# q and k of an attention block loaded whole, from DRAM tiles that span all chunks, in a new order of work

## The chip, the cores and the metric

The kernel runs on one core of a Trainium2 chip. The metric is the device time of one execution in microseconds (us), the lower the better. The engines are named as in the profile: PE (TensorE, matmuls), PEld (its weight loads), DVE (VectorE), ACT (ScalarE), POOL (GpSimd) and SP (SyncE, which here issues every DMA). L249 is line 249 of the kernel before.

## The reference, cut to what matters

```python
# x [1, 2048, 448], wqkv [448, 3*448], wo [448, 448]
# w_gate, w_up [448, 1792], w_down [1792, 448]; 16 heads of 28, window 256
qkv = split_heads(layernorm(x) @ wqkv)          # q, k, v: [16, 2048, 28]
scores = q @ k.T * 28 ** -0.5                   # masked: 0 <= row - col < 256
o = softmax(where(mask, scores, -1e9)) @ v
h = x + merge_heads(o) @ wo
y = layernorm(h)
h2 = h + (gelu(y @ w_gate) * (y @ w_up)) @ w_down
```

All inputs and the output are float32. The kernel splits each float32 operand of a matmul into a high and a low part (ACT makes the high part at L252, DVE or POOL the low part at L255) and adds the three products that matter, so one product of 448 rows takes 11 matmuls.

## The kernel before, in words

The 2048 rows lie in 16 tiles of 128 rows, four tiles to a chunk of 512. The 16 heads lie in four groups of four. A block is one group in one chunk: B from 0 to 15, in two passes of two groups each; chunk c comes after chunk c - 1 within a pass.

**Start.** SP loads the tiles of x (L510), the weights of v in two halves (L583) and those of q and k (L609). Each tile of x is normalised (DVE, POOL), transposed on PE (L320) and split into `xT`. Products of `xT` and the weights of v follow (L249, 128x224). Where PE would be idle at the start, transposes of the identity are issued as fillers (L1315); nothing reads them.

**Projection of q and k** (`project_tile`). For a group and a chunk, 11 matmuls 128x512 fill one PSUM bank, ACT and DVE split it into a high and a low part, and DMAs write the parts to a DRAM tile: two bands in one transfer of 448 KB (L656) and the third in one of 224 KB (L657). A tile of q or k has the shape [112, 3, 512]: 4 heads of 28 rows, three bands (high and low, in an order that makes one product of 84 rows out of the three), 512 columns. Part of k of the last group travels along in pieces of 16 rows (64 and 32 KB).

**Loads** (`loads`, `get`, L678). They bring q and k of a block into SBUF as [84, 4, columns], 84 rows for each of four heads. The buffers `rq` and `rk` are double: block B uses number B % 2. `rk` holds the 256 columns of the chunk before and the 512 of its own. Before, a block takes two loads of q and two of its own k, each of 256 columns (84x4x256, 336 KB), and, if c > 0, one load of the last 256 columns of k of the chunk before. That makes 76 loads of 336 KB, 32 of q and 44 of k.

**Attention of a block.** Scores on PE (L249, `bank<-ring 84*128`, for each head and each tile of 128 queries), their maxima on DVE (L701), the maxima turned round through PE (L728) and back to SBUF, the scores once more with the maximum taken off (L249, `128*128`, out 128x384 or less: called the second scores below), exp on ACT (L775), masking on POOL (L788), the product with v on PE (L807, `29x...`), then wo. The second scores are the last readers of the block's `rq` and `rk`.

**FFN.** From about 306 us on PE has only the products of the FFN and of the last output.

**What sets the order.** The kernel is first recorded as a list of operations with their data; a table of numbers at the end of the file (PLAN) then says in which order each is issued, which PSUM bank it takes and how many fillers go where. No scheduler moves anything afterwards. All DMAs are on SP's one queue and are issued in its order: a transfer whose data or buffer isn't ready holds up all behind it. Eight completion semaphores are used in turn, so a DMA also waits for the eighth before it.

Of the kernel before, what the change touches and what calls it, by code (L numbers as in the profile page):

```python
# [9 lines left out]
F32 = mybir.dt.float32  # L10
# [8 lines left out]
NG = 4  # L19
# [33 lines left out]
MOVED = 16  # L53
QUICK = 4
# [81 lines left out]
def block_kernel(ctx: ExitStack, tc, x, wqk_in, wv_in, wo_in, ffn_in, halves_in, out):  # L136
# [10 lines left out]
    def f(ap):  # L147
# [25 lines left out]
    qk_d = [[[dram.tile([GF, 3, 512], F32, name=f"{'qk'[i]}{g}_{c}") for i in range(2)] for c in range(CS)]  # L173
            for g in range(NG)]
# [461 lines left out]
    def project_tile(p, c, m):  # L636
# [21 lines left out]
        put(slice(0, GF), qk_d[g][c][s], ("d", g, s, c), s, 1)  # L658
        put(slice(GF, 128), qk_d[NG - 1][c][1][16 * m:16 * m + 16], ("d", NG - 1, 1, c, m), 1, 0.15)
# [8 lines left out]
    def loads(B):  # L668
        g, c = block(B)
        u = B % 2  # L670

        def get(s, cc, lo, n, at, key):
            src = qk_d[g][cc][s].rearrange("(j p) b t -> (p b) j t", j=4)[:, :, lo * 128:(lo + n) * 128]
            dst, tok = (rk, "rk") if s else (rq, "rq")
            rd = [(("d", g, 1, cc, m), i) for m in range(WT) for i in range(2)] if s and g == NG - 1 else \
                [(("d", g, s, cc), i) for i in range(2)]
            rd += [("zk" if s else "zq", u, i) for i in range(2)]
            dma(key, 246 * n, lambda: nc.sync.dma_start(f(dst[u][0:3 * DH, :, at * 128:(at + n) * 128]), src),  # L678
                rd, [(tok, u, at + i) for i in range(n)])
# [641 lines left out]
    "c-pOZW3+5L)McEV?QGSxZQHhO+qP}nwr$(CZ5w^wx%KY%`cIG1qkGh-IxES_%3O2J<Rl1C00992aKHeHXfc2zY!cazBCLOYQN%cout22EBP|f&"  # L1321
    "`A-{1{{HEK5iJxM4@O1-k)!`uJaQ(CjP`Hu9}9;)K_rHM5d722B0m3E|KRzvE{(KFI4X+t=8<UrMaTc5_!9|7BIN&B2Sr9BVI(k|+n*MWj0GaU"
    "@IPz(&&Z!l{)s>%W5Y<sU^s6a5f?{{{P94M8K6j1e<GsrY#!+gB6H$l)ch}A6lQ`%VuxXN{)-SrdgI7Z9yy95bHIN+VC2Z3N`gove`><Qys~gr"
    "VR$VR#skAPj6{sW(O6_Yf7W1OE&Sn|MA|US00=V)!ZSb^`=1sJNBx(FKQ*V3xv+3;P?&WTRul{83Bs6pWZ%E>`QLu{w=RDwhQr*kzh53%8~&Fw"
    "5S|Ca8pmPu;6LpA$q|N8;{T|dhqL^5?jK$K?+E^Ifx`*{f1~lRPX6tOVJ{G_G7A6Y;a%`QY_f1%9I3y5IpblSfv`?+*zdnP4*yj#3;VOb9HYO="
    "{i7-vjspMgN*MO#VNOw4-TbdwSR_Z_KlOoOB=B!c{<jt=%o_X8YUr=mAJ+b;6@||v9Nvrnvz!00{_kl5|LzJHRws(oKaM<ycsO$qd8V<jZcyYX"
    "4Obh4D~rQx|LX_C=>9zs{vAQ#)9|11fBXL5{r>lL|Nq7Pzw^T&VT2VY!ipWqNUTWxr-<;?K}wJfq>7l49T*@!hzC-G#2^Yt4|0V5PoFd(CddUc"
    "fM_5GNCq;3v>*iX01qSq=|J-T%*_j;gPb5L$OLkO%Ag9!2daW<zz5Yq4WNLUAT!7hl7bi@%YWvy1_eMH&=#}<?Lh~S6$sD~bOHq<JUWA!unQ;z"
    "x`JAuHmCzk&<)fD^+93K0H~lL2tXsy7&HM*K{L=CXrKis0a}8=U<hahro*8i5s+XQhzo{;5nu+K1((2)U=)}QM}sk78LS7!0t-w5-N8~g6&QFN"
    "=mDmIB49e0180EoU?!La955Tq0TVz^Fc+2urNE>JRCB>{I1$)j9#{ZZz@=arFmW#s4bKP5L2s}EBmjNDLbwRbg9|`$uq0x}N-!U;0xRJ{&=;%*"  # L1330
    "YrrDd4{QS#?hm$u0bnCs1#P?-o&*wS53L1j;U;(*tOEmq3wD6La5Y>HqT|hQAM8!m!9k!H*a>3b^>9B-igtnBz`>`$7PtZK0Y$+9xESmO`@mK>"
    "8SDpZ;5K*woB`XRi(}%xgd-2f!VjT>0(=mDf<E2>Kf|5yAov1z!LP6nsRa6w4d5FbL3YFM@Fd&=AHhT56nqT(lSA+{+z3MWFc4@nh=LEpA8->m"
    "0)N8TxFm>*kHRD12|Na$!ZYw0EDerB6`h4A;B%NBzkui9OL!i>f*0UxcoAL%aquPZ29^UEa7O$K#>bc7d#Ite@G|@jGvO<+JkZfQco|dxFF<B|"
    "1!Rd3{V0+ZR|E#S3a^7~cr?k56W|*l5rpU^_z15-6UD_>!3TI9TBr=T2BM(&Fb9r@ZL}5KfKNa|92Mon(GWs6VJ>_NJ^};CZ5SPmBu~K|h>=8N"
    "$Xyr%Jq85bgE3Jed>_U_x4{E=9t<Q7x&v;4S6~pi0AeE_-2#>I5K;xd1{5X6RdEtLn1oO@TpcHdXTeZ%4lwivxab2IOOAm!s0O|Z-hu?MCLTtT"
    ";#xQ%{0NfaxM&=?2Zj?5b;aXJHyohk_&BJICz2F69-2T>;&&hw?vCT5)c6^A57OWyuntaw(&GDI5=ns4;Vs|+sEeP2qo4<Ff**o}C^P&7GQytt"
    "GZ=}oz@)Gjo=ke<OfV%(jQZeIuqmEGzJO-<8z=y?!oIi&EC|1XemFPIgNwqvI3KQu^W*Oz8*GjX;NPGz{sHRa{+LD_*NM<iP!Q*Xzd%D=2)Drb"
    "VN1+l16&w$SPC}6MX&-PEDc-Xq8LF9o&c?}fI74whBj=2lOq+j#RLXW!ge?WOF$Dwf$gyaU04zp$0cw{Y(Ni|!ck!t+yR%yWpFfD7N>{FkPpk@"
    "@;C#mfQ#W|up&+i3&H5H5>5w;!Opl0EDSs1>@YPPfQ!QzuoEr|hvGD_988JI!yGUL$_XpLTyPj3h%3S2I5!-DW5SWRA{>lI;Z$fU$pc5@)MyMI"
    "f~S#mC@+i!)1bF>I!TYl;@Ge`Ob%PX86+*L569t_a3&dqv!Pj}0jv(QquFE*sS0brxnv&6fvUmzWIWD^YQhDiGR%N#!3j7M%807KqvROLjE<9u"  # L1340
# [170 lines left out]
```

## Time and profile before

| | |
|---|---|
| time, three runs | 675.41, 675.41, 675.98 us; median 675.41 us |
| the profiled execution's own time | 675.42 us |
| its span in the profile | 673.7 us |
| PE busy | 662.4 us (98%), 4074 matmuls |
| DVE, ACT, POOL busy | 511.0, 406.9, 325.1 us |
| loads of q and k | 32 and 44, 336 KB each |
| granted TensorE clock | 1.00 in every stretch to 660 us |

The span is the stretch from the first to the last recorded instruction; 1.7 us of the time lie outside it. "Idle before, releaser" is the time in which an engine had nothing running, and the event that ended it. SPq, POOLq and the like are the sequencers that issue DMAs. The chain of waits goes back from the last instruction, at each step to what released it.

### The profile page before, as it was taken

What the parts mean: (1) busy time and instruction counts of PE and PEld (TensorE: products, weight loads), DVE (VectorE), ACT (ScalarE), POOL (GpSimd) and SP (SyncE); (2) the same over time, 40 slices, a digit from 0 to 9 for tenths busy, and PEclk for the clock granted to TensorE, in tenths of its full rate; (3) what the DMA queues carried; (4) which work ended last, traced back from release to release, by engine and by line L of the source; (5) the groups of instructions that cost most, each with busy time, mean ns of one, the idle gap of its engine ahead of it and who ended that gap; (6) DMA issues with size and microseconds to landing.
All of it is one profiled execution on the core that took longest, in us unless ns stands there. A gap on an engine that the chain in (4) does not pass through costs nothing.

```text
span 673.7 us, 12051 instructions
## 1 busy us (share of the span) xinstructions
PE 662.4 (98%) x4074; PEld 591.8 (88%) x4074; DVE 511.0 (76%) x1287; ACT 406.9 (60%) x793; POOL 325.1 (48%) x506
## 2 busy tenths in 40 slices
PE   7999999999999999999999999999999999999997
PEld 7998888888888888778999899999999989999996
DVE  7887888988778889868897879777775466465464
ACT  4767767787557778976455565556534454543531
POOL 6712445464345458865414654654444563453320
PEclk9999999999999999999999999999999999999999
DMA  8787866666566788643544434323021324122102
GB/s 296 204 257 234 272 203 180 210 190 196 153 188 212 209 207 227 157 112 86 140 108 102 102 96 119 103 91 93 20 71 53 122 68 119 54 67 55 64 15 109
DMA packets 97814, 93.73 MB, mean 139 GB/s; under 512 B 39064, under 2 KB 86360, under 8 KB 97752
## 3 DMA queue, kind: packets, MB, share of 16 engines
q1 hardware_dynamic: 97752, 92.96, 47.3%
q8 instruction: 32, 0.52, 0.3%
q14 instruction: 30, 0.25, 0.1%
HBM read 63.05 MB, written 29.88 MB: 138 GB/s over the span
## 4 chain that ended last, share of the span: by engine, by line
PE 91%; DVE 3%; DMA 2%; SPq 1%; issue 1%; POOL 1%; ACT 1%; DVEq 0%; POOLq 0%
PE bank L249 84%; PE bank L807 6%; DVE bank L701 1%; DMA ring<-k 1%; DMA pp<-in_wv_dram 1%; DMA q<-proj 1%; POOL proj L255 1%; PE bank L320 1%; PE bank L728 0%; DVE mhl L721 0%; ACT pp L775 0%; SPq L657 0%; ACT ring L252 0%; POOL pp L788 0%; SPq L510 0%
## 5 line engine op out<-in xcount | busy, mean ns | idle before, releaser
L249 PE MATMUL bank<-xT,proj 128*128 128x512 f32 x648 | 183.4, 386 | 0.0
L701 DVE CUSTOM_DVE_ANT_0 bank<-bank,mask 128x384 f32<-128x384 f32 (+2 forms) x256 | 131.5, 550 | 23.5 <-PE bank L249 18.4
L249 PE MATMUL bank<-ring 84*128 84x384 f32 (+7 forms) x629 | 140.1, 311 | 1.7 <-DMA ring<-k 0.7
L249 PEld LDWEIGHTS bank<-xT,proj 128*128 128x128 f32 x648 | 118.5, 190 | 12.4 <-issue 0.4
L249 PE MATMUL bank<-xT,ring 128*128 128x512 f32 x508 | 127.5, 379 | 0.0
L249 PE MATMUL bank<-ring,proj 128*128 128x448 f32 x617 | 125.3, 353 | 0.0
L249 PEld LDWEIGHTS bank<-ring,proj 128*128 128x128 f32 x617 | 116.5, 189 | 2.8
L249 PEld LDWEIGHTS bank<-ring 128*128 128x128 f32 (+1 forms) x629 | 106.1, 190 | 12.5 <-ACT pp L775 2.0
L775 ACT ACTIVATE pp<-bank 128x384 f32<-128x384 f32 (+1 forms) x212 | 103.9, 534 | 21.8 <-PE bank L249 18.2
L249 PEld LDWEIGHTS bank<-xT,ring 128*128 128x128 f32 x508 | 95.9, 189 | 12.2 <-DVE v L1022 0.3
L788 POOL TENSOR_SCALAR_AFFINE_SELECT pp<-pp 128x512 f32<-128x512 f32 x120 | 73.3, 639 | 63.1 <-ACT pp L775 61.2
L249 PE MATMUL bank<-proj,xT 128*128 128x224 f32 x352 | 72.6, 268 | 1.1 <-ACT proj L252 1.1
L946 POOL TENSOR_TENSOR raw<-raw 64x128 f32<-64x128 f32 (+1 forms) x110 | 54.9, 510 | 28.7 <-DMA raw<-in_halves_dram 17.1
L249 PEld LDWEIGHTS bank<-proj,xT 128*128 128x128 f32 x352 | 59.4, 191 | 2.3 <-ACT proj L252 1.3
L255 POOL TENSOR_TENSOR ring<-raw,ring 128x256 fp32r<-128x256 f32 (+2 forms) x48 | 43.1, 906 | 35.1 <-ACT ring L252 34.2
L1022 DVE TENSOR_TENSOR v<-v,bank 128x512 f32<-128x512 f32 x48 | 32.8, 683 | 30.6 <-PE bank L249 26.0
L252 ACT ACTIVATE ring<-bank 8x512 fp32r<-8x512 f32 x64 | 37.0, 584 | 24.5 <-PE bank L728 23.6
L255 DVE TENSOR_TENSOR proj<-v,proj 128x512 fp32r<-128x512 f32 (+1 forms) x57 | 38.6, 691 | 17.3 <-ACT proj L252 17.0
L249 PE MATMUL bank<-wos,ohl 128*128 128x448 f32 x192 | 49.3, 359 | 0.1
L252 ACT ACTIVATE proj<-v 128x512 fp32r<-128x512 f32 (+1 forms) x57 | 32.9, 593 | 26.2 <-DVE v L1048 13.6
L1078 DVE TENSOR_TENSOR hres<-bank,hres 128x448 f32<-128x448 f32 x64 | 37.5, 616 | 12.7 <-PE bank L249 12.6
L946 POOL TENSOR_TENSOR v<-raw 128x256 f32<-128x256 f32 x22 | 18.0, 818 | 57.2 <-DMA raw<-in_halves_dram 30.1
(118 smaller groups left out, 1028.9 us busy)
## 6 DMA issues: line engine op xcount, KB each, us to landing
ring<-k SPq DMA_DIRECT2D x44, 336.0 KB
raw<-in_halves_dram SPq DMA_DIRECT2D x22, 640.0 KB
ring<-q SPq DMA_DIRECT2D x32, 336.0 KB
q<-proj SPq DMA_DIRECT2D x15, 448.0 KB
k<-proj SPq DMA_DIRECT2D x11, 448.0 KB
ge<-in_halves_dram SPq DMA_DIRECT2D x20, 224.0 KB
xn<-xn SPq DMA_DIRECT2D x64, 64.0 KB
hres<-in_x_dram SPq DMA_DIRECT2D x16, 224.0 KB
```

The costliest lines, as they stand in the source:

```text
L249: nc.tensor.matmul(o.rearrange("p (t h) -> p t h", h=2), w, mixed(m), **how)
L252: nc.scalar.activation(dst, src, AF.Copy)
L255: (eng or nc.vector).tensor_sub(dst, src, f(hi))
L320: nc.tensor.transpose(bank[b.k][:, n * 128:(n + 1) * 128], xn[i2][:, o:o + 128], ident)
L701: nc.vector.tensor_tensor_reduce(at, at, plain(mask[:, o:384]), 1.0, -BIG, OP.add, OP.max, mx[i // 2][:, i % 2, j:j + 1])
L775: nc.scalar.activation(pp[:, j:j + per, o * 128:o * 128 + n].rearrange("p j (h t) -> p j h t", h=2), bank[b.k][:, 0:n * per].rearrange("p ...
L788: nc.gpsimd.affine_select(a, a, pattern=[[0, 4], [-cm, 128]], compare_op=op_, fill=0.0, base=0, channel_multiplier=cm)
L807: nc.tensor.matmul(bank[b.k][32 * j:32 * j + DH + 1, lo * 128:(hi + 1) * 128], v[:, 4 * c - 2 + m, g % 2, j, :], pp[:, j, at[m] * 128:(at[ ...
L946: op("pool", 0.14 + n * 0.00215, 0.18 + n * 0.00215, key, lambda: nc.gpsimd.tensor_tensor(out, a, b, op=OP.subtract), [*ar, *br], w, port= ...
L1022: op("dve", 0.605, 0.702, key, lambda: nc.vector.tensor_tensor(plain(out), plain(a), unmixed(bank[bs[i].k]), op=OP.add), ar, w, bs[i])
L1078: op("dve", 0.533, 0.626, key + 3 * q + 3, lambda t=t, b=banks[q]: nc.vector.tensor_tensor(plain(hres[:, t, :]), unmixed(bank[b.k][:, 0:D] ...
```

## The change

The DRAM tiles of q and of k span all chunks: one tile [112, 3, 2048] for each group and each of q and k, in place of one [112, 3, 512] for each chunk too. A chunk writes and reads its columns of it. The write of two bands puts down 112x2x512, in pieces of 2 KB a row and band, where it was 112x1024 in one piece of 4 KB. A block's q comes in one load 84x4x512 (672 KB, pieces of 2 KB) in place of two 84x4x256 (pieces of 1 KB), its own k likewise; the load of k of the chunk before stays as it was. There are 44 loads: 16 of q and 28 of k. With that, PLAN is a new table: on every engine operations stand in another order, and the banks have other numbers. The numbers in `LOADS` and the keys belong to the search for the table; once PLAN is there they move nothing. The arithmetic is the same.

```diff
+LOADS = {2: 492, 4: 560, 6: 760}
+ROWS = (((0, 0, 4, 0), (1, 0, 4, 0)), ((1, -2, 2, 0), (0, 0, 4, 0), (1, 0, 4, 0)))
...
-    qk_d = [[[dram.tile([GF, 3, 512], F32, name=f"{'qk'[i]}{g}_{c}") for i in range(2)] for c in range(CS)]
-            for g in range(NG)]
+    qk_d = [[dram.tile([GF, 3, S], F32, name=f"{'qk'[i]}{g}") for i in range(2)] for g in range(NG)]
...
+        at = slice(512 * c, 512 * c + 512)
         def put(rows, d, name, s, size):
-            dma(key, 458 * size, lambda: nc.sync.dma_start(d[:, s:s + 2], both[rows]), tok, [(name, 0)])
-            dma(key, 229 * size, lambda: nc.sync.dma_start(d[:, 2 - 2 * s], both[rows, 0]), tok[0:1], [(name, 1)])
+            dma(key, 458 * size, lambda: nc.sync.dma_start(d[:, s:s + 2, at], both[rows]), tok, [(name, 0)])
+            dma(key, 229 * size, lambda: nc.sync.dma_start(d[:, 2 - 2 * s, at], both[rows, 0]), tok[0:1], [(name, 1)])
...
-        def get(s, cc, lo, n, at, key):
-            src = qk_d[g][cc][s].rearrange("(j p) b t -> (p b) j t", j=4)[:, :, lo * 128:(lo + n) * 128]
+        def get(s, t, n, key):
+            lo = 4 * c + t
+            src = qk_d[g][s].rearrange("(j p) b t -> (p b) j t", j=4)[:, :, lo * 128:(lo + n) * 128]
...
-            dma(key, 246 * n, lambda: nc.sync.dma_start(f(dst[u][0:3 * DH, :, at * 128:(at + n) * 128]), src),
+            dma(key, LOADS[n], lambda: nc.sync.dma_start(f(dst[u][0:3 * DH, :, at * 128:(at + n) * 128]), src),
                 rd, [(tok, u, at + i) for i in range(n)])
         key = 16 * B - (8 if B > 1 else 24)
-        if c:
-            get(1, c - 1, 2, 2, 0, key)
-        for i in range(0, 4, 2):
-            get(0, c, i, 2, i, key + 4 * i)
-            get(1, c, i, 2, 2 + i, key + 4 * i)
+        for s, t, n, k in ROWS[c > 0]:
+            get(s, t, n, key + k)
...
 PLAN = (
-    "c-pOZW3+5L)McEV?QGSxZQHhO+qP}nwr$(CZ5w^wx%KY%`cIG1qkGh-IxES_%3O2J<Rl1C00992aKHeHXfc2zY!cazBCLOYQN%cout22EBP|f&"
+    "c-pPFbGRqD7B*TzC8?y4Qg++6ZEM=L-P5*hyL;NUZQItgZM*yS*}Z4Zx&Ph!eBZ98s=~G2^{zLmU$&;{8r84{HKb|3O5oS?KV|%@9sVklUv2c)"
...
```

The order at the places that the prediction speaks of. A row is a line of the kernel, the operation, its output and inputs, the output's shape, and how many follow one another; the lines of the changed kernel are one to four higher.

First SP at the start of the program, before. `in_x`, `in_wv` and `in_wqk` are x and the weights.

```order
L510 DMA hres<-in_x_dram 128x448 x4
L583 DMA pp<-in_wv_dram 128x448
L609 DMA raw<-in_wqk_dram 128x512
L583 DMA pp<-in_wv_dram 128x448
L510 DMA hres<-in_x_dram 128x448
L609 DMA raw<-in_wqk_dram 128x512
L510 DMA hres<-in_x_dram 128x448 x10
```

The same place in the changed order:

```order
L511 DMA hres<-in_x_dram 128x448 x3
L584 DMA pp<-in_wv_dram 128x448
L511 DMA hres<-in_x_dram 128x448
L584 DMA pp<-in_wv_dram 128x448
L610 DMA raw<-in_wqk_dram 128x512
L511 DMA hres<-in_x_dram 128x448 x7
L610 DMA raw<-in_wqk_dram 128x512
```

Both halves of the weights of v now stand ahead of the first weights of q and k; the fourth tile of x stands behind the first half.

PE at the same place, before: fillers (`bank<-ident`), transposes of x (`ident,xn`), and the first products for v (`proj,xT`).

```order
L1315 MATMUL bank_141<-ident 128x128 x15
L320 MATMUL bank_136<-ident,xn_80 128x128 x4
L1315 MATMUL bank_141<-ident 128x128 x5
L320 MATMUL bank_135<-ident,xn_80 128x128 x4
L249 MATMUL bank_134<-proj,xT 128x224 x7
L320 MATMUL bank_139<-ident,xn_85 128x128 x4
L1315 MATMUL bank_141<-ident 128x128 x5
L249 MATMUL bank_140<-proj,xT 128x224 x8
```

And in the changed order:

```order
L1319 MATMUL bank_117<-ident 128x128 x19
L321 MATMUL bank_110<-ident,xn_80 128x128 x4
L1319 MATMUL bank_117<-ident 128x128 x4
L321 MATMUL bank_117<-ident,xn_80 128x128 x4
L1319 MATMUL bank_116<-ident 128x128 x5
L250 MATMUL bank_112<-proj,xT 128x224 x7
L321 MATMUL bank_115<-ident,xn_85 128x128 x4
L1319 MATMUL bank_116<-ident 128x128
L250 MATMUL bank_110<-proj,xT 128x224 x8
```

Five fillers moved from behind the first seven products for v to before them, and one is left behind.

SP again, at the loads of block 2 (q0 and k0 are group 0), before; q0_1 is q of group 0 in chunk 1.

```order
L678 DMA ring_77<-k0_1_89 84x4x256
L657 DMA k3_2_115<-proj_78 16x512
L678 DMA ring_77<-q0_1_88 84x4x256
L860 DMA raw_79<-in_wo_dram 128x448
L656 DMA k3_2_115<-proj_78 16x1024
L656 DMA k0_2_91<-proj_78 112x1024
L657 DMA k0_2_91<-proj_78 112x512
L657 DMA k3_2_115<-proj_78 16x512
L678 DMA ring_77<-k0_1_89 84x4x256
L678 DMA ring_77<-q0_1_88 84x4x256
```

The same loads in the changed order:

```order
L660 DMA k3_93<-proj_78 16x512
L659 DMA k3_93<-proj_78 16x2x512
L659 DMA q0_86<-proj_78 112x2x512
L685 DMA ring_77<-q0_86 84x4x512
L685 DMA ring_77<-k0_87 84x4x512
L660 DMA k3_93<-proj_78 16x512
L659 DMA k0_87<-proj_78 112x2x512
```

The two pairs of loads, with six other transfers between them, are one pair of twice the size.

PE at the first scores of block 2, before: a product of block 0 with v (`pp,v`), the turned maxima (`one,mhl`), products for later blocks, and in the last row but one the first score of block 2.

```order
L807 MATMUL bank_138<-pp,v 29x384 x8
L807 MATMUL bank_138<-pp,v 29x256 x4
L807 MATMUL bank_138<-pp,v 29x128 x4
L728 MATMUL bank_137<-one,mhl_148 72x128
L249 MATMUL bank_135<-xT,proj 128x512 x2
L728 MATMUL bank_141<-one,mhl_150 72x128
L249 MATMUL bank_135<-xT,proj 128x512 x3
L249 MATMUL bank_134<-ring 128x384
L249 MATMUL bank_140<-proj,xT 128x224
```

In the changed order, from two rows behind that product to the first score of block 2, the last row:

```order
L250 MATMUL bank_116<-proj,xT 128x224
L250 MATMUL bank_110<-ring 128x128
L250 MATMUL bank_116<-proj,xT 128x224
L250 MATMUL bank_111<-xT,proj 128x512
L732 MATMUL bank_113<-one,mhl_124 72x128
L250 MATMUL bank_116<-proj,xT 128x224 x2
L250 MATMUL bank_111<-xT,proj 128x512
L250 MATMUL bank_116<-proj,xT 128x224 x3
L250 MATMUL bank_111<-xT,proj 128x512
L732 MATMUL bank_112<-one,mhl_126 72x128
L250 MATMUL bank_116<-proj,xT 128x224
L250 MATMUL bank_110<-ring 128x384
```

More work stands between the product with v and the first score of block 2: products for v, and scores of block 1.

More of the change, by code (lines that the diff above doesn't have):

```diff
@@ L670, in loads @@
         u = B % 2
-        def get(s, cc, lo, n, at, key):
-            src = qk_d[g][cc][s].rearrange("(j p) b t -> (p b) j t", j=4)[:, :, lo * 128:(lo + n) * 128]
+        def get(s, t, n, key):
+            lo = 4 * c + t
+            src = qk_d[g][s].rearrange("(j p) b t -> (p b) j t", j=4)[:, :, lo * 128:(lo + n) * 128]
             dst, tok = (rk, "rk") if s else (rq, "rq")
-            rd = [(("d", g, 1, cc, m), i) for m in range(WT) for i in range(2)] if s and g == NG - 1 else \
-                [(("d", g, s, cc), i) for i in range(2)]
+            at = t + 2 * s
+            rd = []
+            for cc in range(lo // 4, (lo + n + 3) // 4):
+                rd += [(("d", g, 1, cc, m), i) for m in range(WT) for i in range(2)] if s and g == NG - 1 else \
+                    [(("d", g, s, cc), i) for i in range(2)]
             rd += [("zk" if s else "zq", u, i) for i in range(2)]
-            dma(key, 246 * n, lambda: nc.sync.dma_start(f(dst[u][0:3 * DH, :, at * 128:(at + n) * 128]), src),
+            dma(key, LOADS[n], lambda: nc.sync.dma_start(f(dst[u][0:3 * DH, :, at * 128:(at + n) * 128]), src),
                 rd, [(tok, u, at + i) for i in range(n)])
         key = 16 * B - (8 if B > 1 else 24)
-        if c:
-            get(1, c - 1, 2, 2, 0, key)
-        for i in range(0, 4, 2):
-            get(0, c, i, 2, i, key + 4 * i)
-            get(1, c, i, 2, 2 + i, key + 4 * i)
+        for s, t, n, k in ROWS[c > 0]:
+            get(s, t, n, key + k)
         got[B] = L.ops[-1]
@@ L1326 @@
[L1326 to L1340, printed above, removed]
@@ L1446 @@
[L1446 to L1448 removed]
+    "c-pPFbGRqD7B*TzC8?y4Qg++6ZEM=L-P5*hyL;NUZQItgZM*yS*}Z4Zx&Ph!eBZ98s=~G2^{zLmU$&;{8r84{HKb|3O5oS?KV|%@9sVklUv2c)"
+    "8~iGf$Prp(`|lPQd4b65KP~_1LBF0j@~uVA{ZAkIw+BVeMZemAx53CUB&znGKRwdVe@6VLq(@=^k+uKSag<#YWsOGOFcKGv@&u#2(Z~@X$}Wn;"
+    "OCqEF9o0V;XrvDm83~OX1OF#t7!@0evady=`iB!OvYkf8j(<J%$Y_4!_#GLE9DyQjlSo@6(l3f)8${K9#{we#lSo@2(guw5^4|!+zr2AcA29O$"
@@ new lines @@
+    "J5m&d4E;j#o2lP6w8*GIWDAM1p+#Z%C-dOneA55P7Kvh0i(&;u;`tr#Z><0Dj3Vpce{K|cYf%aTQPKUw_U{b;<{3m`{p|_;%P)+|_CMOwqGp0f"
+    "za;7j{|D=D1;Z$8zx76=u+qpI{mY5=Z=C<|s6}y0{#7uH)F6n$1tQs@Q90A1aFM7vzkPsz_5BYr6s7OqYW<yw-%23=@(TY|F^sZ7qWA<+tL`7R"
+    "|FcGZ`}o~UqT(h|`UO!@(kOf|3OkIP^_w3OrM2Ho;;86<w}B{K&?ws|DvvZO^Z%^$|JnzUy9J1{O{4Y=6ov1<s~!BC6Y}rw@*BxN%BE3_;wVkR"
+    "D8K*c<ezn}MXiE=)B~d!(xNbuNd4m|E`G0G9H}=Nm3#1S{lCn>fA>BTr9k*Ea_xV5{@GW4uY&(t`9B-?|MvTT&+h-fasSCqVlD2kQUWbbWM)yM"
+    "VpD0RmRif9Sy~z`ww6;%s-@NPXt5&xzg+3GP|K(VS_&<bmQTy9rPq{}ON*{0`*(hREv1%Q%kT?J0WF%ASIeR?EoQ_&R~4<Q7E7z9Ro4n?$+a3<"
@@ L1449 @@
+    "RP|N^RddxsHB&8BD>X>{sVb`0s*P%^DyzY&oocVDs3EF@>Zq!!YHFzJqN=MJs-_yIYN<}DwyLA*su8N5>a6Ok25O=jqb8}YYO)%url{d+s+z9G"
+    "slU`THA8h*Gu13LTg_2D)Lb=B%~uOlPqk1jQY+MA)lDr?%hgh~O!;b?+OBq}oobibqxP!ZYM<J#4yc3bkUFeRs3YpAI;M`RlWLV(t;VZ0YOOk}"
+    ")~S_hz1pBQs&i_SI;A$NEo!T}pw6p{>a@C~E~^RZin^+<sq5;Dx}pA7H`Oh5TisE2)jf4zJy#FZL-j~KRxi{O^;Er9&(wSMLA_NU)f@FmeO52k"
+    "7xh(rQ{UAq^+WwsTEsgAB47lHz!7=`iJ%cy1dA{tc!U!nBJ2n=!jF&<ZbT5_Mf^XMu7!#"
 )
```

231 lines of the change are left out of this document (117 added, 114 removed).

## The prediction

> **What bounds the kernel now.** I read the page's busy times and its chain of waits first, then stretches of 20 us, then the start and the loads of q and k in order of time.
>
> ```profile
> PE 662.4 (98%) x4074; PEld 591.8 (88%) x4074; DVE 511.0 (76%) x1287; ACT 406.9 (60%) x793; POOL 325.1 (48%) x506
> PE 91%; DVE 3%; DMA 2%; SPq 1%; issue 1%; POOL 1%; ACT 1%; DVEq 0%; POOLq 0%
> 306.15 362.71 PE bank L249 x1764
> 0.00:20.00 20.00, 16.28 (x101) 14.88 (x102) 14.79 (x33) 10.63 (x18) 12.70 (x31) 1.00 0.76 259
> 20.00:40.00 20.00, 20.00 (x134) 18.62 (x133) 15.76 (x37) 13.29 (x25) 11.42 (x23) 1.00 0.84 247
> 40.00:60.00 20.00, 19.34 (x126) 17.51 (x125) 18.20 (x67) 15.25 (x29) 2.50 (x5) 1.00 0.79 245
> 100.00:120.00 20.00, 19.52 (x148) 16.30 (x146) 18.10 (x60) 15.90 (x33) 10.15 (x14) 1.00 0.63 180
> 160.00:180.00 20.00, 19.38 (x158) 17.09 (x157) 16.05 (x58) 13.96 (x27) 9.45 (x12) 1.00 0.39 115
> 260.00:280.00 20.00, 19.70 (x176) 15.80 (x169) 16.79 (x53) 18.44 (x41) 17.84 (x28) 1.00 0.88 225
> 280.00:300.00 20.00, 19.69 (x142) 16.23 (x141) 17.30 (x54) 15.50 (x35) 10.96 (x18) 1.00 0.46 109
> 480.00:660.00 180.00, 180.00 (x876) 165.06 (x875) 106.69 (x181) 83.79 (x157) 77.80 (x125) 1.00 0.21 65
> 660.00:673.70 13.70, 8.85 (x47) 8.49 (x45) 5.74 (x10) 0.43 (x1) 0.00 (x0) 0.98 0.35 135
> ```
>
> PE is busy 662.4 of 673.7 us and 91% of the chain is its own work. From 306.15 us it runs 1764 products without a pause, 362.71 / 1764 = 0.206 us each; nothing in the change touches these, so gain and loss are to be looked for ahead of 306 us. In the rows of 20 us the first figure behind the comma is PE's busy time: missing are 3.72 us in the first stretch, 0.66 in the third, and 0.48, 0.62, 0.30 and 0.31 in the others shown. The whole idle time of PE is 673.7 - 662.4 = 11.3 us, of which the tail behind 660 us keeps 13.70 - 8.85 = 4.85. So even a perfect order of all before it wins no more than 6.5 us, a little under 1%.
>
> The start, by the time line (the bracket is idle time and its releaser), and the one late load, by the chain and by who waited for the loads' line:
>
> ```profile
> 2.65 0.44 SPq L583 DMA_DIRECT2D pp<-in_wv_dram  x1
> 3.13 0.43 SPq L609 DMA_DIRECT2D raw<-in_wqk_dram  x1
> 7.20 0.58 ACT L252 ACTIVATE proj<-pp 128x448 fp32r<-128x448 f32 x1 [5.13 <-DMA pp<-in_wv_dram]
> 7.68 0.58 ACT L252 ACTIVATE xT<-bank 128x512 fp32r<-128x512 f32 x1
> 9.17 0.58 ACT L252 ACTIVATE proj<-pp 128x448 fp32r<-128x448 f32 x1 [0.91 <-DMA pp<-in_wv_dram]
> 9.80 0.59 PE L249 MATMUL bank<-proj,xT 128*128 128x224 f32 x3 [1.05 <-ACT proj L252]
> 3.61 5.54 DMA pp<-in_wv_dram
> 9.80 1.03 PE bank L249 x7
> 11.27 0.54 PE bank L1315 x5
> 11.81 0.88 PE bank L249 x8
> 49.07 5.70 DMA ring<-k
> 54.90 0.46 PE L249 MATMUL bank<-ring 84*128 84x256 f32 x2 [0.66 <-DMA ring<-k]
>   PE bank L249: 0.7, 1
> ```
>
> The first products for v wait at 9.80 for ACT, and ACT at 9.17 for the second half of v's weights, issued at 3.61 and landed at 9.15 (3.61 + 5.54). And of 76 loads of q and k one was waited for, once (the last row: 0.7 us, 1 time): that of block 1's second half, issued at 49.07, landed 5.70 us later.
>
> **The change part by part.**
>
> *Start: -0.9 us.* Ahead of the second half of v's weights there stood four tiles of x, the first half and one load of wqk; now wqk is behind it. wqk is 128x512 floats, 262 KB, and at the 259 GB/s of the first stretch it takes 1.01 us; the half also goes out one issue (0.48 us) earlier, which lies within that. So it lands at about 8.1. ACT still has its 0.58 us for `xT` at 7.68 ahead of it and starts at 8.27; the first product follows 0.63 us later, as before (9.17 to 9.80): 8.9, 0.9 us sooner. The five fillers moved ahead of it cost 0.54 us of PE, but begin behind transposes that end at about 8.5 or sooner and so end at about 9.0. The next group of eight wants the low part of the same half from POOL; with five fillers less before it, 0.54 us, it can follow. Below: if POOL's low part, behind two steps of the normalisation, comes no more than half a microsecond sooner, the gain is 0.4. Above: landing, ACT and POOL all a whole transfer and slot sooner, 1.3. I take 0.9, since the row of ACT at 9.17 names the DMA alone. The six fillers more on PE (0.11 us each, 0.54 / 5) fill idle time ahead of these products; in the open they would cost 0.65.
>
> *The late load: -0.7 us.* In SP's changed order the whole k and q of block 1 are the 41st and 46th transfer, where the late halves were the 55th and 56th, and the pieces of 16 rows that stood ahead of those come behind. That stall (0.66 us) goes. Bounds: 0.7 won; or 0.7 lost more, if the same stall comes twice as long because all of block 1 now waits for one landing. Next in line is block 2's pair.
>
> *Larger loads, one pair a block: +0.3 us.* SP issues 32 DMAs fewer, by these rows (minimum, median, maximum ns) 32 x 0.39 = 12.5 us of its queue:
>
> ```profile
> L678 SPq DMA_DIRECT2D ring<-k x44: 308/390/1342, 27.1 to 271.9; - x44
> L678 SPq DMA_DIRECT2D ring<-q x32: 309/382/1435, 24.4 to 271.5; - x32
> SPq L678 <- PE bank L249: 59.4, 30, 6.7
> 65.91 2.07 PE bank L807 x32
> 51.71 0.34 PE L249 MATMUL bank<-ring 84*128 84x384 f32 x1
> 51.89 0.26 PE L249 MATMUL bank<-proj,xT 128*128 128x224 f32 x1
> ```
>
> That wins nothing by itself, as nobody waited for that queue but at 54 us. The third row is the point: SP stood 30 times, 2 us on average (59.4 / 30), with its next load, until PE's second scores gave the buffer free. So loads begin on release, and the queue has mostly drained by then. What changes is where a buffer comes free and when it is wanted. Before, the first half of q and k could be fetched while the second half was still read; now the pair waits for the last second score of the block before last, and the first score of the new block for the pair's last byte. Two loads of 336 KB (344 thousand bytes) become two of 672 KB: at 259 GB/s each takes 1.33 us longer, so the pair lands 2.6 us later after its release.
>
> How late is that? The load at 49.07 took 5.70 us with some eight transfers issued just ahead of it; on a queue that has stood for 2 us it takes that much less, 3.7 us (an estimate from these two rows). The second of a pair is issued 0.39 us behind, and the pair carries 2.6 us more: 6.7 us from release to last byte. What covers it, at block 2, are by the order 16 products with v (32 instructions, 2.07 us), 22 products of 224 columns at 0.11 (0.88 / 8), 5 of 512 at 0.206, and 8 scores at up to 0.18 (51.71 to 51.89): 2.07 + 2.42 + 1.03 + 1.44 = 6.96 us, a little less with the short scores, 6.8. The same count gives 6.8 to 8.8 us for the fourteen blocks with a release, eleven of them between 6.8 and 7.5. So the margin is 0.1 to 0.8 us at most of them, a few will be late by a tenth or two: +0.3. Bounds: 0, all hidden; and a pair that takes the whole 5.70 and 2.6 us, 8.3, thus 1.4 us late at fourteen blocks, 20 us. I stay near the lower end because the wait of 2 us before a load is the common case and the drained queue with it.
>
> The Trainium skill, DMA: Bandwidth & Descriptors, section Anatomy of one DMA, says that a transfer's semaphore rises only when its last byte is confirmed, and gives the time as 2.0 us and bytes / 436e3 (fitted for another issuing path). By it 344 thousand bytes more are 0.79 us, a pair lands 1.6 us later and not 2.6, all is hidden, and the sum would be 0.3 us lower. The 259 GB/s of the trace stands against 436, so I keep the row.
>
> *Writes in pieces of 2 KB, not 4: 0.* The bytes are the same, and the loads of the halves come in pieces of 2 KB instead of 1 KB. The DMA engines are busy 0.39 to 0.88 in the rows above, so there is room on both sides; without it, one write of 448 KB takes as long again (1.8 us at 259 GB/s), ahead of loads only.
>
> *The order of the rest: 0, from -2.5 to +2.* The other gaps (0.48, 0.62, 0.30, 0.31 and smaller) come from chains through DVE, ACT and POOL, not from loads. A new order moves each; I have no row that says to which side. Half of the 5 us of idle time between 60 and 306 us won bounds the one side, nearly as much again lost the other.
>
> Sum: 675.42 - 0.9 - 0.7 + 0.3 = 674.1 us for a run like the profiled one. The median is 675.41, so nothing is added.
>
> **The rivals.**
>
> *Late pairs.* One mechanism: the pair of whole loads lands after the work that covers it, at the first scores of a block. For it: margins of 0.1 to 0.8 us, where before the halves left more, and the 5.70 us row. Against: SP's 2 us on a drained queue. It eats the gain of 1.6 us at 0.11 us late per block on average (1.6 / 14), and makes the kernel slower by 0.2% from 0.2 us. If pairs take 0.6 us longer than I say, eleven blocks are late by about 0.4 us: +4.4 in place of +0.3, 678.2 us. By the skill's section just named the pair would be shorter, not longer, so it speaks against this rival.
>
> *A better order all over.* The search also removes half of the other idle time, 2.5 us: 671.6. For it: DVE and ACT are at 76% and 60%, so these gaps come from order, not from load. Against: nothing in the rows names a gap that the change addresses.
>
> *Nothing moves.* The start is bound by POOL, at 0.4, the late load's stall comes back at another block, and the pairs cost their 0.3: about 675.3. For it: three steps of POOL at the start lie between the half's landing and the second group. Against: ACT's row names the DMA.
>
> *The change isn't what it says*, that waits arise because a whole DRAM tile is taken as one piece of data, so that a load waits for writes of later chunks. The loads' order after the writes excludes most of this, and it would show as a wait of several us per block; I give it no share of its own.
>
> **How the numbers follow.** The forecast has 0.5, with its own range 672.9 to 675.3 (0.4 to 1.3 at the start, the late load gone or not, 0 to 1 us for loads, some tenths of order). Late pairs 0.2, better order 0.17, nothing moves 0.13. A difference under 0.2%, 1.35 us, can't be told from none here. The forecast's -1.3 lies just on that bound: half of it, 0.25, counts as faster, 0.25 as same. Better order adds 0.17 to faster, nothing moves 0.13 to same, late pairs 0.2 to slower. By halves of a border that I can't place I give 0.44, 0.36 and 0.2. The range is 671.6 to 677.6: it ends at the better order's price, and short of the late pairs', so that about half of each of these two, 0.18 together, is left out.
>
> **What would show it.** In the changed profile: the first 128x224 product at 8.9 rather than 9.80, still released by ACT's high part of v's weights; no wait for a load of k or q near 54 us; 44 loads, 16 of q and 28 of k. For the larger loads, the row of who waited for the loads' line: up to five waits with under 0.5 us in total by the forecast, ten or more with 3 us and up by the first rival. Between 60 and 306 us PE's busy time in stretches of 20 us would be short by 2 to 4 us in all; by the second rival by under 2. From about 305 us on, 1764 products at 0.206 us. I am wrong if the first product doesn't come sooner, if any pair is waited for by more than 0.5 us, or if products of the same form take another time than before.

## The result, and the profile after

| | before | changed |
|---|---|---|
| time, median | 675.48 us (675.41 to 675.98, 4 runs) | 706.36 us (704.12 to 712.41, 4 runs) |
| ratio | | 1.0469, 95% interval 1.0405 to 1.0534 |
| the profiled execution | 675.42 us, span 673.7 | 712.41 us, span 710.7 |

The kernel became 4.7% slower, 31 us by the medians and 37.0 us by the two profiled executions. The forecast was 674.1 us. The page of the changed kernel: engines with their busy time, the clock granted to PE in 40 slices, and the shares of the chain that ended last.

```profile
PE 678.1 (95%) x4080; PEld 608.1 (86%) x4080; DVE 514.4 (72%) x1287; ACT 407.5 (57%) x793; POOL 325.2 (46%) x506
...
PEclk9999999888999999989999999999999999999999
...
PE 80%; DMA 12%; ACT 3%; issue 2%; DVE 1%; SPq 1%; POOL 1%; DVEq 0%; ACTq 0%; POOLq 0%
```

DMA went from 2% to 12% of the chain. The sum is simple. PE's idle time went from 11.3 to 710.7 - 678.1 = 32.6 us, 21.3 more, and its busy time from 662.4 to 678.1, 15.7 more, for the same products and six fillers: 37.0 together. Busy time grew because the clock fell, as the second line shows by its eights.

Next the waits of PE in the changed kernel: total us, times, longest.

```profile
PE bank L250 <- issue: 9.1, 5, 2.5
PE bank L250 <- DMA ring<-q: 7.4, 4, 2.8
PE bank L250 <- DMA ring<-k: 6.3, 5, 1.9
```

Nine waits name a load of q or k, 13.7 us. One of them, 0.5 us at 37.63 us, is at the first score of block 0; the other eight stand at first scores of later blocks. Five more, 9.1 us, have no named releaser ("issue") and stand at the first score of a block too, as one of them shows below. Block 15's first score, at 314.44 us, waits for 1.5 us as well, which the view puts down to ACT. Together these are 14 pauses, one for each block from the third on, 0.3 to 2.8 us long and 23.7 us in all. The completion events in the trace (the times at which a transfer reports that its bytes have landed) show that all 14 are waits for the loads: each of these scores begins 0.04 to 0.14 us after the second load of its pair has landed. By the view of the line of the loads, the nine named waits are what others waited for:

```profile
  PE bank L250: 13.7, 9
```

The chain that ended last shows the loads in it, each with its start and the time to its landing, and the start of the last long stretch:

```profile
78.78 8.04 DMA ring<-k
...
95.79 7.89 DMA ring<-k
...
131.05 8.19 DMA ring<-q
...
166.82 9.29 DMA ring<-q
...
186.63 7.95 DMA ring<-q
...
261.88 8.84 DMA ring<-k
...
344.01 362.38 PE bank L250 x1764
```

These are second loads of their pairs, at six different blocks: 7.9 to 9.3 us each, where the one late load in the kernel before took 5.70. The 1764 products at the end take 362.38 us, as before (362.71), but begin at 344.01 in place of 306.15, so all of the loss lies ahead of them.

The loads go out on release. Here is SP's wait for PE in front of the line of the loads, in the changed kernel (total us, times, longest):

```profile
SPq L685 <- PE bank L250: 70.8, 21, 10.1
```

Block 3, by the time line of SP and PE:

```profile
78.41 0.31 SPq L685 DMA_DIRECT2D ring<-q  x1
78.78 0.43 SPq L685 DMA_DIRECT2D ring<-k  x1
...
85.16 0.65 PE L250 MATMUL bank<-xT,proj 128*128 128x512 f32 x2
...
86.95 0.40 PE L250 MATMUL bank<-ring 84*128 84x384 f32 x1 [1.15 <-DMA ring<-k]
```

The load of q goes out at 78.41, that of k at 78.78, and k lands at 86.82 (78.78 + 8.04), 8.4 us after the pair's start. PE has done all it had by 85.81 and stands for 1.15 us. Over the 14 blocks, by the completion events, a pair takes 8.3 to 10.3 us from its first issue to its last byte; PE's other work lasts 6.7 to 8.7 us from the same moment.

And the clock. PE's time line at the block of 120 us:

```profile
118.60 0.49 PE L250 MATMUL bank<-ring 128*128 128x256 f32 x3
120.76 4.51 PE L250 MATMUL bank<-ring 84*128 84x384 f32 x17 [1.67 <-issue]
```

The same place in stretches of 4 us: behind the stretch its length, then busy time and instructions of PE, PEld, DVE, ACT and POOL, the granted clock, DMA's share, GB/s.

```profile
116.00:120.00 4.00, 3.09 (x52) 1.61 (x43) 3.55 (x12) 2.57 (x5) 0.73 (x2) 1.00 0.88 224
120.00:124.00 4.00, 3.24 (x15) 3.27 (x15) 2.63 (x8) 2.35 (x5) 1.25 (x2) 0.68 0.88 299
124.00:128.00 4.00, 4.00 (x13) 3.45 (x13) 3.10 (x14) 2.55 (x6) 2.03 (x3) 0.50 0.50 172
128.00:132.00 4.00, 4.00 (x25) 3.96 (x24) 2.98 (x9) 3.40 (x8) 1.89 (x4) 0.97 0.30 72
```

After a pause of 1.67 us PE works at half speed until about 128 us: 13 matmuls in 4 us where 25 follow in the next. The trace's clock records of this execution have seven such stretches between 120 and 325 us, three of 6.83 us and four of 3.41, 34.1 us in all; at half speed that costs 17 us, about what PE's busy time grew by.

### The profile page after: what moved, and what is told of

The parts are those of the page before. It is cut to its first block, busy times and chain, and to the rows that moved or that the text cites. A ratio compares the mean times of both kernels' runs of the same rounds, so it can differ in the third digit from the quotient of the medians.

```text
span 710.7 us, 11999 instructions
## 1 busy us (share of the span) xinstructions
PE 678.1 (95%) x4080; PEld 608.1 (86%) x4080; DVE 514.4 (72%) x1287; ACT 407.5 (57%) x793; POOL 325.2 (46%) x506
## 4 chain that ended last, share of the span: by engine, by line
PE 80%; DMA 12%; ACT 3%; issue 2%; DVE 1%; SPq 1%; POOL 1%; DVEq 0%; ACTq 0%; POOLq 0%
PE bank L250 76%; DMA ring<-k 6%; DMA ring<-q 5%; PE bank L811 3%; ACT pp L779 1%; PE bank L321 1%; DMA hres<-in_x_dram 1%; ACT ring L253 1%; DMA q<-proj 1%; DVE bank L705 1%; DMA k<-proj 0%; SPq L660 0%; POOL proj L256 0%; PE bank L732 0%; ACT proj L253 0%
## 5 line engine op out<-in xcount | busy, mean ns | idle before, releaser
L250 PE MATMUL bank<-xT,proj 128*128 128x512 f32 x648 | 180.3, 386 | 0.1
L250 PE MATMUL bank<-ring 84*128 84x384 f32 (+7 forms) x629 | 146.2, 327 | 24.3 <-issue 9.1
L250 PEld LDWEIGHTS bank<-ring 128*128 128x128 f32 (+1 forms) x629 | 113.9, 204 | 34.3 <-issue 19.8
L250 PE MATMUL bank<-proj,xT 128*128 128x224 f32 x352 | 63.6, 285 | 0.2 <-POOL e L538 0.2
L250 PE MATMUL bank<-wos,ohl 128*128 128x448 f32 x192 | 52.1, 381 | 0.0
L250 PE MATMUL bank<-X,ring 128*128 128x512 f32 x138 | 45.5, 379 | 0.0
```

Of the source, the lines that this page charges most:

```text
L250: nc.tensor.matmul(o.rearrange("p (t h) -> p t h", h=2), w, mixed(m), **how)
```

## The experiments

Theory W: a block's pair of whole loads can't start until the whole buffer is free and lands 8.3 us after that or later, while PE has 6.8 to 7.5 us of other work at most blocks (the prediction's count); the pauses then pull the clock down. Each run is compared with the kernel before on the same chip.

**The layout alone undone.** DRAM tiles cut by chunk again, order and whole loads as changed.

```diff
-    qk_d = [[dram.tile([GF, 3, S], F32, ...
+    qk_d = [[[dram.tile([GF, 3, 512], F32, ...
-            src = qk_d[g][s].rearrange("(j p) b t -> (p b) j t", j=4)[:, :, lo * 128:(lo + n) * 128]
+            src = qk_d[g][lo // 4][s].rearrange("(j p) b t -> (p b) j t", j=4)[:, :, lo % 4 * 128:(lo % 4 + n) * 128]
```

> The changed kernel and its order, with the DRAM tiles of q and k cut by chunk again (two-band writes in one piece of 4 KB a row, rows 2 KB apart); loads stay whole. Theory W (whole loads begin only when the whole buffer is free, so each pair lands about 8.4 us after its release against 6.8 to 7.5 us of cover, and PE's pauses bring its clock down): the 14 pauses of 1.2 to 2.8 us stay, 700 to 710 us. Rival L (rows 8 KB apart in DRAM make the transfers slow): a first load lands 4.4 us after its issue instead of 5.4, the pauses go, 674 to 678 us.

704.24 us against 674.89, ratio 1.044 (1.0398 to 1.0482). The pauses stay, 22.9 us at the first scores of the same 14 blocks where it was 23.7, so the rows that lie 8 KB apart are not the cause.

**The layout alone.** The kernel before with tiles over all chunks.

```diff
-    qk_d = [[[dram.tile([GF, 3, 512], F32, ...
+    qk_d = [[dram.tile([GF, 3, S], F32, ...
-            ... nc.sync.dma_start(d[:, s:s + 2], both[rows]) ...
+            ... nc.sync.dma_start(d[:, s:s + 2, 512 * c:512 * c + 512], both[rows]) ...
```

> The kernel before in its own order and with its 76 loads of halves, only the DRAM tiles of q and k span all chunks, and the two-band writes go in pieces of 2 KB. Theory W: 675 to 676.5 us, no difference that can be measured. Rival L: loads land a microsecond later than before (median 5.0 us from issue), and pauses come at several blocks: over 680 us.

674.96 us against 674.89, ratio 1.0001 (0.9986 to 1.0016). The layout and the writes in shorter pieces cost nothing; rival L, the layout as the cause, is out from both sides.

**Whole loads alone.** The kernel before, its order and layout, with own q and k loaded whole where the later half stood.

```diff
+                elif s in half:
+                    nc.sync.dma_start(f(dst[u][0:3 * DH, :, 2 * s * 128:(2 * s + 4) * 128]),
+                                      qk_d[g][cc][s].rearrange("(j p) b t -> (p b) j t", j=4))
+                else:
+                    half.add(s)
```

> The kernel before, its order and its DRAM tiles, with own k and q of a block loaded whole at the place of the later of their two halves. The work on PE between a block's last second score two blocks earlier and its first score is 4.9 to 8.3 us here. Theory W (a pair lands 8.5 us after the release, whatever the order): pauses of 8.5 minus that cover, 30 us over fourteen blocks, and 10 to 25 us more for the low clock: 715 to 732 us. Rival O (the new order of the other engines is what costs): 675 to 680 us.

758.06 us against 675.24, ratio 1.123 (1.120 to 1.126), above what theory W gave. Its waits of PE:

```profile
PE bank L249 <- DMA ring<-q: 27.3, 7, 7.7
PE bank L249 <- DMA ring<-k: 22.6, 6, 5.8
PE bank L249 <- issue: 6.0, 2, 3.8
```

That is 56 us and not 30: with the old order other transfers stand between q and k of some blocks, so their second load is issued late too (at one block q goes out at 114.73 and k at 117.57). The direction is plain. The new order of the other engines is not what costs: with it whole loads cost 31 us, without it 83. How much of that difference is its longer cover, and how much its pairs that go out together, these runs don't separate.

**The loads cut into halves, the changed kernel otherwise.** First halves of q and k at the place of the first whole load, second halves at that of the second.

```diff
+        def half():
+            i = 2 * len(calls)
+            calls.append(i)
+            for dst, at, src in whole:
+                nc.sync.dma_start(f(dst[u][0:3 * DH, :, (at + i) * 128:(at + i + 2) * 128]),
+                                  src[:, :, i * 128:(i + 2) * 128])
...
+            dma(key, LOADS[n], half if n == 4 else ...
```

> The changed kernel and its order, but each pair of whole loads is issued as four halves of 336 KB at the two places: first halves of q and k at the first, second halves at the second. Theory W: the first halves land 3.1 and 4.4 us after the first issue, as pairs of halves did before, so 2 us before they are wanted; the second halves land at about 7.0 and are wanted 2 us after the first; all 14 pauses go, and with them the low clock: 673.5 to 675.5 us. Rival L: halves from rows 8 KB apart land no sooner than 5 us; pauses of a microsecond stay, over 690 us.

674.88 us against 674.89, ratio 0.9995 (0.9972 to 1.0018): the whole 30 us are gone, with start, order, layout and the place of the first issue unchanged. Among what PE still waits for:

```profile
PE bank L250 <- DMA ring<-k: 2.3, 2, 2.1
...
PE bank L321 <- ACT xn L311: 1.3, 1, 1.3
```

The one long wait for a load, 2.1 us, is at block 10, by PE's time line:

```profile
194.55 0.46 PE L250 MATMUL bank<-ring 84*128 84x384 f32 x2 [2.07 <-DMA ring<-k]
```

**Halves in the wrong order.** Both halves of one tensor, then both of the other.

```diff
+            def load():
+                for i in range(0, n, 2):
+                    nc.sync.dma_start(f(dst[u][0:3 * DH, :, (at + i) * 128:(at + i + 2) * 128]),
+                                      src[:, :, i * 128:(i + 2) * 128])
+            dma(key, LOADS[n], load,
```

> The changed kernel, each whole load issued as two halves at its own place: both halves of the one tensor, then both of the other, so that what the first score needs is the first and the third of four halves. Theory W: where first halves come first, the third half lands about 7.6 us after the first issue, 8 us after the release against 6.8 to 7.5 us of cover at most blocks; pauses of 0.3 to 1.1 us at about ten blocks, less than half of those with whole loads, and one to three stretches of low clock: 680 to 688 us. Rival S (a large transfer is slow in itself, and any cut into halves cures it): 673.5 to 676 us.

679.07 us against 675.24, ratio 1.0056 (1.0038 to 1.0073): between the two expectations, a little under theory W's. The waits, 5.6 us in six places, are fewer than I said, and the stretches of low clock that I expected did not come: the clock records are full from 6.19 to 675.21 us.

```profile
PE bank L250 <- DMA ring<-q: 2.6, 2, 1.8
PE bank L250 <- DMA ring<-k: 1.8, 3, 0.9
PE bank L250 <- issue: 1.2, 1, 1.2
```

The same bytes in the same pieces at the same place: what the first score needs is then the third to land and no longer the second, and that costs 4 us (ratio 1.0056 against 0.9995). Most of the cure, some 27 of 31 us, thus comes with the cut in either order, since the first score no longer needs the last byte of the pair; the order of the bytes is worth the rest. That the pieces themselves are no faster is seen at block 3: by the completion events its third half lands 7.3 us after the first issue and its fourth 8.5 us, as late as the whole pair.

**Work for PE in the pauses.**

```diff
         def one():
+            if B > 1 and B not in filled:
+                filled.add(B)
+                for _ in range(16):
+                    nc.tensor.transpose(bank[b.k][:, 0:128], ident, ident)
```

> The changed kernel with 16 transposes of the identity on PE (0.11 us each, 1.8 us, read by nobody) ahead of the first score of each block from the third on, so that PE works while the loads are late. Theory W with the clock as a result of the pauses: granted clock 1.00 throughout, the 17 us of half speed won, what 1.8 us exceed the shorter pauses lost (about 3 us): 688 to 694 us. Rival C (the clock comes down for a reason other than the pauses): clock still 0.97 to 0.98, 706 to 712 us.

697.77 us against 674.89, ratio 1.034 (1.0301 to 1.0378). Its span with the mean granted clock:

```profile
core 0: 693.9 us, clock 1.000
```

And the stretches that had been at 0.68 and 0.50, with the columns as above:

```profile
120.00:124.00 4.00, 3.85 (x27) 3.12 (x24) 2.63 (x9) 2.83 (x6) 1.71 (x3) 1.00 0.91 265
124.00:128.00 4.00, 3.81 (x22) 3.59 (x23) 3.97 (x17) 3.80 (x9) 1.81 (x2) 1.00 0.69 222
```

The loads come as late as before (block 3's pair 8.5 us after its first issue), PE only does something useless meanwhile, and the clock doesn't fall. Rival C, a clock that falls for another reason than the pauses, is out. The time is above the range I gave. The 224 transposes take 26.8 us by the profile's groups of instructions, 0.12 us each, which is more than the 22.9 us that the run is slower than the kernel before. Against the changed kernel's 706.36, measured on another chip, it is 8.6 us better; since the fillers run on where a pause was short, the clock costs about that or more there.

**The price of the loads by itself.** A series of loads behind the kernel's last work, each group waiting for the one before.

```diff
+    for _ in range(2):
+        load(0, 0, 2)
+        load(0, 0, 4)
+        load(0, 0, 2), load(1, 0, 2)
+        load(0, 0, 4), load(1, 0, 4)
+        load(0, 0, 2), load(1, 0, 2), load(0, 2, 2), load(1, 2, 2)
+        load(0, 0, 4), load(1, 0, 4), write(0), write(1)
```

> The changed kernel with a series of loads behind its last work, each group waiting for the one before, nothing else on the queue but the last outputs: one half (336 KB), one whole (672 KB), a pair of halves, a pair of wholes, four halves, and a pair of wholes with two writes of 448 KB behind it; all twice. The extra time of the run means nothing. My estimate in the forecast (1.33 us for 336 KB more): from the first issue 3.1, 4.4, 4.4, 7.0 us, four halves 7.0, and the same 7.0 with the writes behind. Theory G (a load costs more than that whatever is behind it): pair of wholes and four halves 8 us or more alone too. Theory F (writes issued behind the pair share the engines with it): 7 us alone, 8 us or more with the writes.

SP's time line. An issue follows within 0.1 us of the landing it waits for, so starts can be read as landings: the pair of halves out at 706.42 and 706.78, each landed where the whole load of the same tensor goes out, 709.83 for q and 711.02 for k, and so on.

```profile
706.42 0.31 SPq L1325 DMA_DIRECT2D ring<-q  x1
706.78 0.43 SPq L1325 DMA_DIRECT2D ring<-k  x1
709.83 0.31 SPq L1325 DMA_DIRECT2D ring<-q  x1
711.02 0.31 SPq L1325 DMA_DIRECT2D ring<-k  x1
715.16 0.31 SPq L1325 DMA_DIRECT2D ring<-q  x1
718.59 0.31 SPq L1325 DMA_DIRECT2D ring<-k  x1
```

A half takes 3.4 us (706.42 to 709.83), one whole load by itself 5.2 (701.22 to 706.40, by the completion events), a pair of halves 4.6 (to 711.02), a pair of wholes 709.83 to 718.59 = 8.8 us. The second series gives 5.0 us for one whole, 4.5 and 8.8 for the pairs. With two writes of 448 KB behind it the pair took 8.6 and 8.2 us by the completion events.

The pair of wholes isn't quite clean. Each load waits only for the one before it into the same buffer, so q's whole load went out while k's half was still on its way, and k's whole load went out 1.2 us behind q's, where it was 0.36 in the pair of halves: up to 0.8 of the 8.8 us are this late issue. For the same reason the four halves didn't go out together (the first 3.4 us ahead of the rest) and give no price.

Theory G stands: doubling the pair costs 4.2 us, or 3.4 without the late issue, not 2.7. Theory F falls: what is issued behind a pair doesn't slow it. The stretch of the pair of halves, and that in which both whole loads were on their way (PE, PEld, DVE, ACT and POOL, the granted clock, DMA's share, GB/s):

```profile
706.40:711.00 4.60, 0.00 (x0) 0.00 (x0) 0.00 (x0) 0.00 (x0) 0.00 (x0) 0.50 0.57 154
711.00:718.60 7.60, 0.00 (x0) 0.00 (x0) 0.00 (x0) 0.00 (x0) 0.00 (x0) 0.50 0.87 222
```

While both whole loads were under way the DMA engines were 0.87 busy and moved 222 GB/s, not 259. Why the rate stays there isn't shown.

**The start alone.** The kernel before with one swap in SP's order.

```diff
+        words[sp[5]], words[sp[6]] = words[sp[6]], words[sp[5]]
```

> The kernel before with one swap in its order: the second half of the weights of v is issued ahead of the first load of wqk. My term of 0.9 us: first product of v at 8.9 us instead of 9.80, and 0.9 us off the whole, 674.0 us. Rival P (POOL's low part of that half, which comes behind two steps of the normalisation, sets the second group of products): first product at 8.9 us, yet the stream of products starts no more than 0.5 us sooner, 0 to 0.5 us off the whole.

674.83 us against 675.24, ratio 0.9992 (0.9979 to 1.0006). It fits 0 to 0.5 us better than 0.9, but the interval holds both. In this profile the first half of the weights itself landed late, at about 8.0 us in place of 7.2, the first product came at 9.61, and the long stream of products began at 13.26, no sooner than in the kernel before (13.00).

**First halves as early as they can.** Each first half issued as soon as its own data and its own half of the buffer allow.

```diff
+            for i in range(0, n, 2):
+                o = dma(key, LOADS[n], lambda i=i: nc.sync.dma_start(...
+                if i < n - 2:
+                    L.first.append(o)
...
+            for e in [e for e in first if e.deps <= done]:
+                e.fn()
```

> The changed kernel with all loads as halves, and each first half issued as soon as its data are written and its own half of the buffer has been read, instead of after the last second score of the block. Theory W: no pause for a load at the first scores, no low clock, the start of the new order kept: 672.5 to 674.5 us against 674.9 for the kernel before on the last chip. Rival N (the new order has other waits that the late loads hid): 675 to 678 us.

686.29 us against 675.24, ratio 1.0158 (1.0133 to 1.0183): much slower. Both expectations missed it, the rival less. The largest part is one chain at the start of the attention; beside it the trace has a pause of 2.4 us for a load of q at 201.03 and two stretches of 3.41 us at half clock, one behind each of the two pauses. The idle time that PE and ACT had, by their time line:

```profile
54.92 0.60 ACT L260 ACTIVATE proj<-bank 128x512 fp32r<-128x512 f32 x1 [6.16 <-DMA k<-proj]
...
56.22 1.12 PE L328 MATMUL bank<-ident,xn 128*128 128x128 f32 x4 [5.76 <-ACT xn L318]
```

And the chain up to there; L693 is the line of the loads, L666 and L667 are those of the writes of q and k:

```profile
48.67 1.25 SPq L693
...
49.96 0.70 SPq L666
...
50.70 0.42 SPq L667
...
51.17 0.42 SPq L667
...
51.63 3.27 DMA k<-proj
...
54.92 0.02 ACT proj L260
...
55.42 0.76 ACT xn L318
```

PE waits 5.76 us for a normalisation on ACT; ACT stands 6.16 us in front of that with a copy into a projection buffer, which comes free only when a write of k has read it; and that write stands in SP's one queue behind a load whose issue took 1.25 us and three other writes. The loads now stand early, in the middle of the writes. A load that goes out too early can cost as much as one that is late.

**Two versions drawn from this.** With block 1's pair left whole, since halves there held back the same chain (the 1.3 us for `ACT xn` above):

```diff
-            if n == 4:
+            if n == 4 and B != 1:
                 whole.append((dst, at, src))
```

> The changed kernel with pairs issued as four halves, as in the run of that name, but block 1's pair left whole: with halves the eight loads in flight at 44 to 50 us held back writes, ACT and the transposes of x, a pause of 1.29 us that the changed kernel doesn't have there. Theory W with that detail: 1.3 us less than with all halves, 673 to 674.5 us where the kernel before gives 674.9 to 675.2. Rival V (such pauses come and go with the chip's transfers and cancel over runs): no difference to the kernel before, 674.5 to 675.5 us.

674.94 us against 674.95, ratio 1.0014 (0.9994 to 1.0034): no difference, as rival V said. Its runs spread widely, though: five of twelve took 677.4 to 680.3 us, the profiled one (678.07) among them, and why isn't known. The single pause did shrink, to 0.55 us in its profile, but the one at block 10 remained. Block 10's first scores are not of the first tile, by PE's order: they need both halves of k and the second of q.

```diff
+            todo = [(*w, i) for w in whole]
+            if B == 10:
+                (q, k) = sorted(whole, key=lambda w: w[0] is rk)
+                todo = [(*q, 2), (*q, 0)] if i else [(*k, 0), (*k, 2)]
+            for dst, at, src, i in todo:
```

> As the run before it (all pairs but block 1's as four halves), with block 10's halves in the order in which the new order of work wants them: its first scores are of the last tile and need both halves of k and the second of q, so k's two, then q's second, then q's first. Before, the half that they waited for came fourth: a pause of 2.0 us and 3.4 us at half clock behind it, 3.7 us together. Theory W: the third half lands about 0.9 us sooner, the pause is 1 us or less, the clock stays: 672.5 to 674.2 us, 0.1 to 0.3% under the kernel before. Rival V (pauses come and go and cancel over runs): 674.5 to 675.5 us.

672.80 us against 675.00, ratio 0.9970 (0.9956 to 0.9985). It is faster than both kernels, by 0.3% than the one before, as theory W said. The largest of PE's waits:

```profile
PE bank L321 <- ACT xn L311: 1.7, 1, 1.7
```

No row of that view names a load of q or k any more. In its chain the last stretch starts so:

```profile
304.74 362.38 PE bank L250 x1764
```

That is 1.4 us sooner than in the kernel before (306.15). It is not less idle time: PE is busy for 55.66 of the first 60 us here and for 55.62 before, and for 242.01 us between 60 and 304 us against 241.89. The clock records become full at 5.52 us here and at 7.48 before, which may be a part of it. How much of the gain is the start and how much the order can't be told from these runs.

## Why the prediction was wrong, point by point

**Where to look** was right: nothing happened behind the start of the last 1764 products, and the loss lies at the first scores of the blocks. **The start** came as said for the first product, and for less than said in the stream, by PE's time line of the changed kernel:

```profile
8.77 1.24 PE L250 MATMUL bank<-proj,xT 128*128 128x224 f32 x7
...
11.69 0.36 PE L250 MATMUL bank<-proj,xT 128*128 128x224 f32 x1 [0.24 <-POOL e L538]
...
12.50 2.24 PE L250 MATMUL bank<-proj,xT 128*128 128x224 f32 x18
```

8.77 us, forecast 8.9; the second half of v's weights landed at 8.11, forecast 8.1. But one product of the second group waits for POOL until 11.69, and the long stream begins at 12.50 where it began at 13.00: 0.5 us, near the lower bound of 0.4 which named POOL, not the 0.9 I took. **The late load** at 54 us is gone, as said, but the first score of block 0 now waits 0.5 us for its k (at 37.63), which the kernel before doesn't have: of the 0.7 us little was won.

**The larger loads** are the step that failed, and the failure is of size. The mechanism, a pair that waits for the last second score and lands behind the work that covers it, was the first rival, with 0.2. The cover was counted right: 6.8 to 8.8 us, measured 6.7 to 8.7. The pair was not. I put its last byte 6.7 us after the release: 3.7 us for a half on a drained queue, 0.39 for the second issue and 2.6 for the double size at 259 GB/s. In the kernel it took 8.3 us at the quickest and 10.3 at block 13. By terms, with the probe's times: 3.4 us for the half, 1.2 for the second load of the pair (4.6 - 3.4), and 3.7 for the double size (8.3 - 4.6; 4.2 in the probe). So of the 1.6 us that were missing from 6.7 to 8.3 the double size is 1.1 and the second load 0.8, less 0.3 for the first. I had taken a mean rate of a stretch with many transfers in flight as the price of one more load. That the 3.7 came near 3.4 was luck: SP's wait of 2 us taken off the time of one transfer is no price of another. The upper end I had worked out, 8.3 us and 1.4 us late at fourteen blocks, was nearly the truth: 23.7 us over 14 pauses are 1.7 us each. I set it aside since SP's waits of 2 us showed a drained queue. At block 3 the queue was drained (the transfer before the pair had landed at 78.19, the pair went out at 78.41), and the pair still took 8.4 us: a drained queue made only the first term small.

**The clock** was in no term. I priced a pause at its own length. In the profiled execution the fourteen pauses of 1.7 us brought 21.3 us more idle time and another 15.7 us of slow work, so even the upper bound of 20 us was too low by almost half of what came. The experiment with fillers shows that the second part hangs on the first.

**Writes of 2 KB at 0** was right, by the layout run. **The order of the rest** at 0 fits what the last version shows: between 60 and 304 us PE is idle for 2.1 us in the kernel before and for 2.0 there. The bound of 2.5 us, half of 5 us of idle time, was a slip: of the 11.3 us the tail has 4.85, the first stretch 3.72 and the late load 0.66, which leaves 2.1. So the rival of a better order all over had no 2.5 us to win, and that the last version comes near its 671.6 us doesn't confirm it. **The range** ended at 677.6 because I held the late pairs to be 0.6 us later than my estimate at most; the upper bound of that very term, 20 us in place of 0.3, would have put its end at 675.42 - 0.9 - 0.7 + 20 = 694.

## What to carry to other kernels

Where a double buffer is refilled, count from the last read that frees it to the first read of the new data, and hold against that the landing of the last byte that this first read needs; merging two transfers into one turns "the first half" into "all of it". Take the price of a transfer from one of that size, or from two issued together, not from a mean rate. A pause of PE that comes back in every block is to be priced with the slow work behind it, and bytes that are wanted first should be issued first, but not so early that they stand ahead of writes that others wait for.

## What the runs showed of the hardware that I had not expected

PE's clock falls to half after pauses well under two microseconds, and stays there for 3.41 or 6.83 us (once for 10.24, in the kernel before with whole loads). Counted over all profiles in stretches of 3.41 us that begin where the clock records change: with less than 1.3 us of idle time in a stretch the clock never fell behind it, with more than 2.0 us it always did where it had been full, and between 1.35 and 1.95 both occur. A pause that is split over two stretches can be harmless: the one of 2.45 us ahead of 214.38 in the changed kernel, one of those with no slow work behind it, is of that kind. The Trainium skill, TensorE: Matmul & The Clock Gate, section Why this matters for your kernels, says to avoid idle gaps of more than about 3 us. The runs agree that the clock is set by windows, and differ in the size: about half a window of idle time can be enough.

Loads are not priced by the byte alone, nor at the mean rate of a busy stretch: by the probe 336 KB took 3.4 us, twice that in two loads 4.6, and four times that 8.8 us (up to 0.8 of it a late issue), with nothing else on the queue but the end of the load before. In the kernel with halves, four of 336 KB needed as long as two of 672 KB (by the completion events in the traces 8.5 us from the first issue to the last landing at block 3, 77.16 to 85.68, against 8.4), so it is the amount in flight and not the size of the piece. Why the second half of these bytes takes more time than the first stays open.
